# Joining the tiled stages of a Nyströmformer attention: R, A and both C v groups in one stage, R and C v in one PSUM bank, denominators earlier, G in two stages, u of two batches in one tile

## The chip, the cores and the metric

One core of one Trainium2 chip. The metric is the device time of one execution in microseconds (us). Runs of a program on one core are called slow when they lie over 1.5% above the fastest of the same kernel, the others called fast. "Span" is the time between the first and the last instruction of the profiled execution, some 1 to 2 us under its device time.

The engines: TensorE (PE, with its weight loads as PEld), VectorE (DVE), ScalarE (ACT), GpSimd (POOL), SyncE (SP, which here only issues transfers). Matmuls write into PSUM; "bank" is used here for 512 fp32 columns of it, the size of the code's `small` and `acc` tiles. "Start to start" below means from the start of one group of matmuls to the start of the next, so that waits and entries are included.

## The reference, cut to what matters

```python
# q, k, v: (8 batches, 8 heads, 576, 64)
q_lm = q.reshape(B, H, 32, 18, D).mean(axis=3)        # landmarks; k_lm alike
A  = softmax(q @ k_lm.T);  Bm = softmax(q_lm @ k_lm.T);  C = softmax(q_lm @ k.T)
Z  = Bm.T / (norm1(Bm) * norminf(Bm))
for _ in range(6):
    Z = 2 * Z - Z @ Bm @ Z                            # approximate inverse
x = (A @ Z @ C @ v), heads side by side               # (4608, 512)
out = ((x @ w1) * (x @ w2)) @ w3 @ w_out              # d_ff 1024
```

## The kernel before: the parts that matter

w3 and w_out are folded into one matrix `w34` at the start, and the attention of batch 0 is woven into that fold. After it, batch b does its up products (`g` against the normalised A: 8 `j`, two products each) and its down products ("chunks", `ab` against `w34`), and the attention of batch b+1 is woven in between: a Python generator, one stage per `yield`. The order of the matmuls is set by hand, and the timelines below show TensorE running them in that order, so a stage is a run of small matmuls between two runs of large ones. Most stages use the array as several small tiles (`tile_position`); up and down products use it whole. Counts of matmuls are those of the trace, in which an fp32 matmul call appears as two instructions (the 8 calls of R are x16 in the timelines below).

```python
def big():    return psp.tile([128, 2, 512], FP32, name="big", bufs=3)    # two PSUM banks each
def small():  return psp.tile([128, 512], FP32, name="small", bufs=1)     # one bank
def acc():    return psp.tile([128, 512], FP32, name="acc", bufs=1)       # one bank

# ... inside attention(st, bank); bank is small for batch 0, acc later ...
psR = bank()
# R: 16 matmuls of 32x32 into psR
for qd in range(2):                        # four VectorE reads of R in all
    nc.vector.tensor_scalar(out=sz_[:, qd, 0:32], in0=psR[:, 32*qd:32*qd+32], ...)
    nc.vector.scalar_tensor_tensor(out=tz_[:, qd, :], in0=psR[:, 32*qd:32*qd+32], ...)
scores_a(0)
yield
scores_a(1)

def cv(qd, es, psV):
    for r in range(6):
        for h in range(4): nc.tensor.matmul(psV[32*h:32*h+32, 0:64], ects[qd]..., vt...)   # L305
    for h in range(4): nc.tensor.matmul(psV[32*h:32*h+32, 64:65], es..., ones...)          # L310
    nc.vector.reciprocal(out=rcr, in_=psV[:, 64:65])
    nc.vector.tensor_scalar(out=sz_[:, qd, 32:96], in0=psV[:, 0:64], scalar1=rcr, ...)

cv(0, es0, small())
yield
cv(1, es1, bank())
yield
# ... (helpers cut: denominators() fills one half of a big(), inverted() and mixed()
#      turn it into rmix, the reciprocals of A's denominators; normalise() multiplies A by it)
for it in range(6):
    # 16 matmuls of the inverse, copies by VectorE (tz_, sz_)
    if it == 1: psS = denominators()
    elif it in (2, 3, 4): inverted(it - 2)
    elif it == 5: rmix = mixed()
    yield
# psZ, zt
normalise(0, rmix)
yield
normalise(1, rmix)
for n in range(2):
    for w in range(2):
        # G: 16 matmuls of 64x512, evicted by ScalarE or VectorE
        yield
```

The later loads are issued per batch: at its start four transposing loads (`turn_all`) and, behind them on the same queue, v as one block of 1152 KB; after the up products q and k, on GpSimd's queue.

The softmax here doesn't subtract the row's maximum and nothing guards it: scores larger than these inputs give would overflow.

Of the kernel before, what the change touches and what calls it, by code (L numbers as in the profile page):

```python
# [31 lines left out]
def kernel(  # L32
# [145 lines left out]
    def attention(st, bank=None):  # L178
# [102 lines left out]
                                 func=AXF.Exp, scale=SCALE / GRP)  # L281
            eat.append(e)

        psR = bank()
        for qd in range(2):
            for h in range(4):
                sl = slice(32 * h, 32 * h + 32)
                nc.tensor.matmul(psR[sl, 32 * qd:32 * qd + 32], bt[sl, qd, :], bt[sl, qd, :],
                                 start=True, stop=True, tile_position=(32 * h, 32 * h))
        sz_ = pz.tile([128, 2, 96], FP32, name="sz_")  # L290
        tz_ = pz.tile([128, 2, 32], FP32, name="tz_")
        for qd in range(2):
            nc.vector.tensor_scalar(out=sz_[:, qd, 0:32], in0=psR[:, 32 * qd:32 * qd + 32],
                                    scalar1=nrn[:, qd:qd + 1], scalar2=None, op0=ALU.mult)
            nc.vector.scalar_tensor_tensor(
                out=tz_[:, qd, :], in0=psR[:, 32 * qd:32 * qd + 32], scalar=nrn[:, qd:qd + 1],
                in1=eye2[:, qd, :], op0=ALU.mult, op1=ALU.add)
        scores_a(0)
        yield
        scores_a(1)  # L300

        def cv(qd, es, psV):
# [11 lines left out]
            nc.vector.tensor_scalar(out=sz_[:, qd, 32:96], in0=psV[:, 0:64],  # L314
                                    scalar1=rcr[:, 0:1], scalar2=None, op0=ALU.mult)


        cv(0, es0, small())
        yield
        cv(1, es1, bank())  # L320
        yield


        ahat = []
        psS = None

        def denominators():
            ps = big()
            for qd in range(2):
                for c in range(4):  # L330
                    nc.tensor.matmul(ps[32 * c:32 * c + 32, 0, 0:QS],
                                     onesq[:, qd].rearrange("p a b h -> p (a b h)"),
                                     eat[qd][:, QS * c:QS * (c + 1)],
                                     start=(qd == 0), stop=(qd == 1), tile_position=(0, 32 * c))
            return ps

        def inverted(i):
            sl = slice(QS // 3 * i, QS // 3 * (i + 1))
            nc.vector.reciprocal(out=psS[:, 1, sl], in_=psS[:, 0, sl])

        def mixed():
            rr = psS[:, 1, 0:QS]
            rhi = pat.tile([128, QS], FP16, name="rhi", bufs=1)
            nc.vector.tensor_copy(out=rhi, in_=rr)
            rmix = pat.tile([128, QS], FP16, name="rmix")
            nc.vector.scalar_tensor_tensor(out=rmix, in0=rhi, scalar=lomask[:, 0:1], in1=rr,
                                           op0=ALU.mult, op1=ALU.add)
            return rmix

        def normalise(qd, rmix):  # L350
            psD = big()
            for c in range(4):
                nc.tensor.matmul(psD[:, c // 2, QS * (c % 2):QS * (c % 2) + QS],  # L353
                                 selc[:, qd, c, :], rmix[:, :], start=True, stop=True)
            a = pat.tile([128, 2, HS], FP16, name="ahat", bufs=4)
            nc.vector.tensor_tensor(out=a, in0=eat[qd].rearrange("p (c s) -> p c s", c=2),  # L356
                                    in1=psD[:, :, 0:HS], op=ALU.mult)
            ahat.append(a)


        for it in range(6):
            last = it == 5
            psI = big()
            o = 32 if last else 0
            for h in range(4):
                for qd in range(2):
                    sl = slice(32 * h, 32 * h + 32)
                    t = h ^ qd
                    nc.tensor.matmul(psI[32 * t:32 * t + 32, qd, o:96], tz_[sl, qd, :],  # L369
                                     sz_[sl, qd, o:96], start=True, stop=True,  # L370
                                     tile_position=(32 * h, 32 * t))
            if not last:
                tz_ = pz.tile([128, 2, 32], FP32, name="tz_")
                nc.vector.tensor_tensor(out=tz_, in0=psI[:, :, 0:32], in1=eye2, op=ALU.add)
                sz_ = pz.tile([128, 2, 96], FP32, name="sz_")
                nc.vector.tensor_copy(out=sz_, in_=psI[:, :, 0:96])
            else:
                xd = pz.tile([128, 2, 64], FP32, name="xd")
                nc.vector.tensor_copy(out=xd, in_=psI[:, :, 32:96])
            if it == 1:  # L380
                psS = denominators()
            elif it in (2, 3, 4):
                inverted(it - 2)
            elif it == 5:
                rmix = mixed()
            yield
        psZ = small()
        for qd in range(2):
# [5 lines left out]
        nc.scalar.activation(out=zt[:, 0], in_=pzv, func=AXF.Copy, scale=-ZS)  # L394
        nc.vector.scalar_tensor_tensor(out=zt[:, 1], in0=pzv, scalar=-ZS, in1=zt[:, 0],
                                       op0=ALU.mult, op1=ALU.subtract)
        normalise(0, rmix)
        yield
        normalise(1, rmix)
        st["ahat"] = ahat  # L400


        g = st["g"] = pat.tile([128, 2, 2, DF], FP16, name="gt")
        for n in range(2):
            for w in range(2):
                psG = big()
                fs = slice(512 * n, 512 * n + 512)
                for i in range(2):
                    for h in range(4):
                        for qd in range(2):  # L410
                            rs = slice(64 * qd, 64 * qd + 64)
                            nc.tensor.matmul(psG[32 * h:32 * h + 32, qd, :], zt[rs, i, h, :],  # L412
                                             wup[rs, h, w, fs], start=(i == 0), stop=(i == 1),
                                             tile_position=(64 * qd, 32 * h))
                if w == 0:
                    nc.scalar.activation(out=g[:, :, w, fs], in_=psG, func=AXF.Copy, scale=1.0 / ZS)  # L416
                else:
                    nc.vector.tensor_scalar(out=g[:, :, w, fs], in0=psG, scalar1=1.0 / ZS,  # L418
                                            scalar2=None, op0=ALU.mult)
                yield  # L420

    def up(st, j, w):
        p = big()
# [6 lines left out]
            nc.scalar.copy(out=st["a_sb"], in_=p[:, :, 0:HS])  # L430
        else:
            nc.vector.tensor_tensor(  # L432
                out=st["ab"][:, j, :].rearrange("p (c s) -> p c s", c=2),
                in0=st["a_sb"], in1=p[:, :, 0:HS], op=ALU.mult)


    rows = out.rearrange("(b p g) f -> b g p f", b=B, g=6)

    def down(srcs, half, hold, bank):
        if half == 0:  # L440
            hold["ps"] = bank()
        pso = hold["ps"]
        for j in range(4 * half, 4 * half + 4):
            o = 0
            for _, ab, s0, sz in srcs:
                nc.tensor.matmul(pso[o:o + sz, :], ab[:, j, s0:s0 + sz], w34[:, j, :],  # L446
                                 start=(j == 0), stop=(j == 7),
                                 tile_position=(0, o))
                o += sz
        if half == 1:  # L450
            o_sb = po.tile([128, DM], FP32, name="o_sb")
            nc.scalar.activation(out=o_sb, in_=pso[:, :], func=AXF.Copy,  # L452
                                 scale=1.0 / (X64 * X64))
            o = 0
            for b, _, s0, sz in srcs:
                while sz:
                    gi, p0 = divmod(s0, NP)
                    n = min(sz, NP - p0)
                    nc.sync.dma_start(out=rows[b, 2 * (gi % 3) + gi // 3, p0:p0 + n, :],
                                      in_=o_sb[o:o + n, :])  # L460
                    o, s0, sz = o + n, s0 + n, sz - n


    def fold(pf, wof, w3f, wsp):
# [58 lines left out]
    with tc.tile_pool(name="pf", bufs=2) as pf:  # L523
# [19 lines left out]
        load_wout(2, nc.scalar)  # L543
        load_w3(1, 1)

        warm = pf.tile([128, 512], FP16, name="warm", bufs=1)
        nc.vector.memset(warm, 0.0)
        psw = big()
        for _ in range(10):
            nc.tensor.matmul(psw[:, 0, :], warm[:, 0:128], warm, start=True, stop=True)  # L550

        nc.gpsimd.tensor_copy(out=gate, in_=wof[1][:, 0, 0:1])
        load_qk(sts[0], 0)
# [25 lines left out]
        load_w3(5)  # L579
        steps(fd, 4)  # L580
        at = attention(sts[0])
        for n, m in enumerate((2, 2, 2, 2, 2, 2, 2, 1, 1, 1, 1, 1, 1, 1, 2, 2, 2, 2, 2, 1)):
            steps(at)
            if n == 3:
                load_w3(6)
# [7 lines left out]
            steps(fd, m)  # L593
        steps(at, 30)
        steps(fd, 64)
    pab = ctx.enter_context(tc.tile_pool(name="pab", bufs=3))
    at = attention(sts[1], acc)


    for b in range(B):  # L600
        st = sts[b]
        ab = st["ab"] = pab.tile([128, 8, S], FP16, name="ab")
        if b + 2 < B:
            turn_all(b + 2)
            load_v(sts[b + 2], b + 2)
        if b % 2 == 0:
            chunks = [[(b, ab, 128 * t, 128)] for t in range(4)]
        else:
            chunks = [[(b - 1, sts[b - 1]["ab"], 512, 64), (b, ab, 0, 64)]]
            chunks += [[(b, ab, 64 + 128 * t, 128)] for t in range(4)]  # L610
        for j in range(8):
            up(st, j, 0)
            steps(at, (0, 0, 1, 1, 1, 1, 1, 2)[j] if b == 0 else 1)
            up(st, j, 1)
        if b + 3 < B:
            load_qk(sts[b + 3], b + 3)
        if b + 2 < B:
# [4 lines left out]
        nd = 2 * len(chunks)  # L622
        for n in range(nd):
            bank = (lambda: big()[:, 0, :]) if n // 2 % 2 else acc
            down(chunks[n // 2], n % 2, hold, bank)
            steps(at, 2 if n == 6 and nd == 8 or b == 0 and n > 3 else 1)
        steps(at, 30)
        steps(nxt)
        at = nxt


# [28 lines left out]
```

## Time and profile before

| | before |
|---|---|
| device time, median (lowest to highest) | 296.15 us (295.37 to 296.77), 3 runs |
| span of the profiled run | 294.9 us |
| two batches of the main loop (up products of batch 2 to those of batch 4) | 56.07 us |
| TensorE waits marked "issue" | 0.40 us, once |

The first fence is from the page of the kernel before: the span, the busy time and its share for each engine, the chain of work that ended last by engine.

```profile
span 294.9 us, 9448 instructions
...
PE 277.5 (94%) x4026; PEld 152.7 (52%) x4026; DVE 174.1 (59%) x442; ACT 123.7 (42%) x199; POOL 141.7 (48%) x184
...
PE 82%; DVE 9%; ACT 6%; issue 2%; DVEq 0%; ACTq 0%
...
q8 instruction: 31, 0.51, 0.7%
```

TensorE bounds it (busy 94% of the span, 82% of the chain). But the ends of matmuls are modelled, so busy time also covers short waits (below, R is listed with 0.33 us and the next group starts 0.26 after it); start-to-start times are the better measure. The next fence is the PE timeline of the kernel before, in the batch that starts at 190.8 us: start, duration, engine, line, operands, array tile, shape, count, and in brackets an idle time with what ended it.

```profile
196.48 0.33 PE L288 MATMUL acc<-bt 32*32 32x32 f32 x16
196.74 0.32 PE L274 MATMUL big<-qkT,lm 64*32 64x288 f16 x8
196.99 1.15 PE L426 MATMUL big<-ahat,gt 128*128 128x288 f16 x8
198.07 0.32 PE L274 MATMUL big<-qkT,lm 64*32 64x288 f16 x8
198.32 0.88 PE L305 MATMUL small<-vt,ect 96*32 96x64 f32 x48
199.01 0.22 PE L310 MATMUL small<-ones,es 96*32 96x1 f32 x8
199.16 1.15 PE L426 MATMUL big<-ahat,gt 128*128 128x288 f16 x8
200.25 0.88 PE L305 MATMUL acc<-vt,ect 96*32 96x64 f32 x48
200.94 0.22 PE L310 MATMUL acc<-ones,es 96*32 96x1 f32 x8
201.09 1.15 PE L426 MATMUL big<-ahat,gt 128*128 128x288 f16 x8
...
210.17 1.04 PE L446 MATMUL acc<-w,ab 128*128 128x512 f16 x4
211.14 0.44 PE L389 MATMUL small<-bmbd,xd 128*64 128x128 f32 x4
...
211.77 1.03 PE L446 MATMUL acc<-w,ab 128*128 128x512 f16 x4
212.63 0.41 PE L353 MATMUL big<-rmix,selc 128*128 128x144 f16 x4
212.98 0.62 PE L412 MATMUL big<-wup,zt 64*32 64x512 f16 x16
213.53 1.04 PE L446 MATMUL big<-w,ab 128*128 128x512 f16 x4
```

Two things to see. Four down products (L446) take 0.97 us before a tiled group and 0.86 before one that uses the whole array: an entry into tiled work cost about 0.10 us. So it is throughout the main loop of this trace, from 80 us on: 0.95 to 0.99 us in 47 places before tiled groups, 0.86 to 0.88 in 9 before whole-array ones. And R with A0, A1 with the first C v, and the second C v are three stages: 0.51, 1.09 and 0.84 us, without any wait, plus three entries.

The last fence is from the list of PE's waits (line and what it waited for: total us, times, longest).

```profile
PE big L426 <- ACT a_sb L430: 1.7, 8, 0.2
PE acc L199 <- ACT lm L188: 1.4, 6, 0.3
PE big L369 <- issue: 0.4, 1, 0.4
```

### The profile page before, as it was taken

How to read it: one execution, taken by the hardware profiler on the slowest of the kernel's cores; microseconds unless marked ns; L12 is line 12 of the kernel's file. 1: busy time of each engine (PE TensorE's matmuls, PEld its weight loads, DVE VectorE, ACT ScalarE, POOL GpSimd, SP SyncE). 2: the span in 40 equal slices, each digit the busy share in tenths (PEclk: the TensorE clock that was granted, in tenths of full speed). 3: DMA queues.
4: the chain of work that ended last, by engine and by line, in shares of the span. 5: the costliest groups of instructions: out<-in, count | busy, mean ns of one | idle time of the engine just before them, and what ended most of it. 6: DMA issues, size and time to landing. Idle time of an engine off the chain costs nothing.

```text
span 294.9 us, 9448 instructions
## 1 busy us (share of the span) xinstructions
PE 277.5 (94%) x4026; PEld 152.7 (52%) x4026; DVE 174.1 (59%) x442; ACT 123.7 (42%) x199; POOL 141.7 (48%) x184
## 2 busy tenths in 40 slices
PE   8799789999999899999999999999999999999993
PEld 3355346544575357436743764376457435744641
DVE  7843733374474676656765765476666665665720
ACT  2114234215272366146525732573266236625531
POOL 1705405097049929942993599059909931500000
PEclk9799979999999999999999999999999999999999
DMA  7899999919956849947996999389949532012124
GB/s 238 279 235 242 219 259 259 182 35 178 175 133 87 186 104 186 210 132 111 175 227 165 146 224 189 100 167 203 221 116 169 119 107 71 4 37 74 37 65 113
DMA packets 61385, 45.56 MB, mean 154 GB/s; under 512 B 34976, under 2 KB 53408, under 8 KB 61344
## 3 DMA queue, kind: packets, MB, share of 16 engines
q1 hardware_dynamic: 46896, 31.86, 49.2%
q0 software_dynamic: 13632, 11.54, 25.0%
q10 hardware_dynamic: 816, 1.57, 1.5%
q8 instruction: 31, 0.51, 0.7%
q14 instruction: 10, 0.08, 0.1%
HBM read 38.80 MB, written 9.44 MB: 164 GB/s over the span
## 4 chain that ended last, share of the span: by engine, by line
PE 82%; DVE 9%; ACT 6%; issue 2%; DVEq 0%; ACTq 0%
PE big L426 17%; PE acc L446 13%; PE acc L490 12%; PE big L446 10%; PE big L412 6%; DVE ab L432 4%; PE big L369 4%; ACT a_sb L430 3%; PE small L305 2%; PE big L477 2%; PE small L490 2%; PE acc L305 2%; PE big L224 2%; PE big L550 2%; PE big L353 1%
## 5 line engine op out<-in xcount | busy, mean ns | idle before, releaser
L426 PE MATMUL big<-ahat,gt 128*128 128x288 f16 x512 | 74.1, 286 | 2.5 <-ACT a_sb L430 1.7
L432 DVE TENSOR_TENSOR ab<-a_sb,big 128x576 f16<-128x576 f16 x64 | 48.0, 750 | 19.6 <-PE big L426 8.4
L426 PEld LDWEIGHTS <-gt 128*128 128x128 f16 x512 | 47.1, 98 | 19.1 <-issue 4.1
L430 ACT CAST a_sb<-big 128x576 f16<-128x576 f32 x64 | 41.0, 640 | 36.7 <-PE big L426 35.9
L235 POOL TENSOR_TENSOR t<-ect 96x384 f32<-96x384 f32 x16 | 15.9, 994 | 79.3 <-ACT ect L228 78.6
L490 PE MATMUL acc<-wsp,w3t 128*128 128x512 f16 x168 | 43.4, 394 | 5.4 <-DVE w3t L483 2.7
L446 PE MATMUL acc<-w,ab 128*128 128x512 f16 (+1 forms) x192 | 41.0, 382 | 0.1
L446 PEld LDWEIGHTS <-ab 128*128 128x128 f16 (+1 forms) x320 | 24.0, 100 | 32.7 <-issue 9.8
L446 PE MATMUL big<-w,ab 128*128 128x512 f16 x128 | 32.8, 381 | 0.2 <-DVE ahat L356 0.2
L490 PEld LDWEIGHTS <-w3t 128*128 128x128 f16 x192 | 18.4, 101 | 25.9 <-issue 6.7
L166 POOL TENSOR_TENSOR tr<-qkT 128x768 f32<-128x768 f16 x15 | 24.6, 1642 | 11.5 <-DMA qkT<-qkn 6.6
L418 DVE TENSOR_SCALAR gt<-big 128x1024 f16<-128x1024 f32 x16 | 19.6, 1225 | 17.9 <-PE big L412 17.9
L452 ACT ACTIVATE o_sb<-acc 128x512 f32<-128x512 f32 x20 | 11.9, 597 | 38.5 <-PE acc L446 35.7
L167 POOL TENSOR_TENSOR tr<-tr,qkT 128x768 f32<-128x768 f32 x15 | 24.6, 1641 | 1.2
L483 DVE SCALAR_TENSOR_TENSOR w3t<-big,w3t 128x512 f16<-128x512 f32 x16 | 11.1, 691 | 18.9 <-ACT w3t L482 18.9
L482 ACT ACTIVATE w3t<-big 128x512 f16<-128x512 f32 x16 | 9.5, 596 | 25.6 <-PE big L477 20.7
L416 ACT ACTIVATE gt<-big 128x1024 f16<-128x1024 f32 x16 | 16.4, 1024 | 7.9 <-PE big L412 7.9
L412 PE MATMUL big<-wup,zt 64*32 64x512 f16 x512 | 19.3, 381 | 0.0
L452 ACT ACTIVATE o_sb<-big 128x512 f32<-128x512 f32 x16 | 9.6, 597 | 21.8 <-PE big L446 21.8
L228 ACT ACTIVATE ect<-big 96x768 f32<-96x768 f32 x16 | 12.9, 807 | 3.3 <-PE big L224 2.9
L356 DVE TENSOR_TENSOR ahat<-eat,big 128x576 f16<-128x576 f16 x16 | 11.9, 749 | 1.2 <-PE big L353 1.2
L172 POOL TENSOR_TENSOR o<-o,tr 128x256 f32<-128x256 f32 x15 | 12.0, 800 | 1.2
(313 smaller groups left out, 358.5 us busy)
## 6 DMA issues: line engine op xcount, KB each, us to landing
vt<-in_v_dram SPq DMA_DIRECT2D x8, 1152.0 KB, 8.7
qkn<-in_k_dram POOLq DMA_DIRECT2D x8, 576.0 KB, 10.5
qkn<-in_q_dram POOLq DMA_DIRECT2D x8, 576.0 KB, 13.2
out_dram<-o_sb SPq DMA_DIRECT2D x24, 192.0 KB, 2.3
w3f<-in_moe_w_dram SPq DMA_DIRECT2D x6, 512.0 KB, 8.0
out_dram<-o_sb SPq DMA_DIRECT2D x24, 128.0 KB, 2.3
wup<-in_moe_w_dram POOLq DMA_DIRECT2D x4, 512.0 KB, 18.4
wof<-in_moe_w_out_dram ACTq DMA_DIRECT2D x3, 512.0 KB, 7.5
```

The source lines that it names most:

```text
L166: eng.tensor_tensor(out=tr, in0=x[:, :, 0, :], in1=x[:, :, 1, :], op=ALU.add)
L167: eng.tensor_tensor(out=tr, in0=tr, in1=x[:, :, 2, :], op=ALU.add)
L235: nc.gpsimd.tensor_tensor(out=t3[0:NP], in0=e[:, :, 0:3, :], in1=e[:, :, 3:6, :], op=ALU.add)
L412: nc.tensor.matmul(psG[32 * h:32 * h + 32, qd, :], zt[rs, i, h, :], wup[rs, h, w, fs], start=(i == 0), stop=(i == 1), tile_position=(64 * ...
L416: nc.scalar.activation(out=g[:, :, w, fs], in_=psG, func=AXF.Copy, scale=1.0 / ZS)
L418: nc.vector.tensor_scalar(out=g[:, :, w, fs], in0=psG, scalar1=1.0 / ZS, scalar2=None, op0=ALU.mult)
L426: nc.tensor.matmul(p[:, c, 0:HS], st["g"][:, qd, w, 128 * j:128 * j + 128], st["ahat"][qd][:, c, :], start=(qd == 0), stop=(qd == 1))
L430: nc.scalar.copy(out=st["a_sb"], in_=p[:, :, 0:HS])
L432: nc.vector.tensor_tensor(out=st["ab"][:, j, :].rearrange("p (c s) -> p c s", c=2), in0=st["a_sb"], in1=p[:, :, 0:HS], op=ALU.mult)
L446: nc.tensor.matmul(pso[o:o + sz, :], ab[:, j, s0:s0 + sz], w34[:, j, :], start=(j == 0), stop=(j == 7), tile_position=(0, o))
L452: nc.scalar.activation(out=o_sb, in_=pso[:, :], func=AXF.Copy, scale=1.0 / (X64 * X64))
L490: nc.tensor.matmul(psW[j][:, :], turned[j, c // 4][:, a, c % 4, :], wsp[:, b, c, :], start=(c == 0 and a + b == 0), stop=(c == 7 and a == 1))
```

## The change

Its intent: fewer changes between whole-array and tiled matmuls. R, A and both C v become one stage. R and both C v share one `small` bank (`psX`) with the denominators and their reciprocals (the scores of A stay in `big`); the denominators go beside the first inverse step; the normalisations beside the fifth and sixth; G runs in two stages; `ab` of two batches is one tile, so a straddling chunk (64 rows of one batch and 64 of the next) needs no column tiles. The stage counts between the large products are adapted.

```diff
-        psR = bank()
+        psX = small()
...
-                nc.tensor.matmul(psR[sl, 32 * qd:32 * qd + 32], bt[sl, qd, :], bt[sl, qd, :],
+                nc.tensor.matmul(psX[sl, 140 + 32 * qd:172 + 32 * qd], bt[sl, qd, :], bt[sl, qd, :],
...
         scores_a(0)
-        yield
         scores_a(1)
...
-        cv(0, es0, small())
+        cv(0, es0, psX)
+        cv(1, es1, psX[:, 72:137])
         yield
-        cv(1, es1, bank())
-        yield
... denominators() writes psX[:, 208:352], the reciprocals go to psX[:, 352:496]
-            if it == 1:
-                psS = denominators()
-            elif it in (2, 3, 4):
-                inverted(it - 2)
-            elif it == 5:
-                rmix = mixed()
+            if it == 0:
+                denominators()
+            elif it < 4:
+                inverted(it - 1)
+                if it == 3:
+                    rmix = mixed()
+            else:
+                normalise(it - 4)
             yield
... (psZ, zt)
-        normalise(0, rmix)
         yield
-        normalise(1, rmix)
... (in G: the yield moves from the inner to the outer loop)
-    pab = ctx.enter_context(tc.tile_pool(name="pab", bufs=3))
+    pab = ctx.enter_context(tc.tile_pool(name="pab", bufs=2))
... one ab of 2 * S columns for two batches; down() takes 128 columns of it
-            steps(at, (0, 0, 1, 1, 1, 1, 1, 2)[j] if b == 0 else 1)
+            steps(at, (0, 0, 1, 1, 1, 1, 0, 1)[j] if b == 0 else (1, 1, 1, 1, 0, 1, 0, 0)[j])
... warm-up: 20 matmuls of 256 columns for 10 of 512; other stage counts
```

More of the change, by code (lines that the diff above doesn't have):

```diff
@@ L292, in attention @@
         for qd in range(2):
-            nc.vector.tensor_scalar(out=sz_[:, qd, 0:32], in0=psR[:, 32 * qd:32 * qd + 32],
+            psR = psX[:, 140 + 32 * qd:172 + 32 * qd]
+            nc.vector.tensor_scalar(out=sz_[:, qd, 0:32], in0=psR,
                                     scalar1=nrn[:, qd:qd + 1], scalar2=None, op0=ALU.mult)
             nc.vector.scalar_tensor_tensor(
-                out=tz_[:, qd, :], in0=psR[:, 32 * qd:32 * qd + 32], scalar=nrn[:, qd:qd + 1],
+                out=tz_[:, qd, :], in0=psR, scalar=nrn[:, qd:qd + 1],
                 in1=eye2[:, qd, :], op0=ALU.mult, op1=ALU.add)
         scores_a(0)
-        yield
         scores_a(1)
@@ L315, in cv @@
                                     scalar1=rcr[:, 0:1], scalar2=None, op0=ALU.mult)
-        cv(0, es0, small())
+        cv(0, es0, psX)
+        cv(1, es1, psX[:, 72:137])
         yield
-        cv(1, es1, bank())
-        yield
-        ahat = []
-        psS = None
         def denominators():
-            ps = big()
             for qd in range(2):
                 for c in range(4):
-                    nc.tensor.matmul(ps[32 * c:32 * c + 32, 0, 0:QS],
+                    nc.tensor.matmul(psX[32 * c:32 * c + 32, 208:208 + QS],
                                      onesq[:, qd].rearrange("p a b h -> p (a b h)"),
@@ L334, in denominators @@
                                      start=(qd == 0), stop=(qd == 1), tile_position=(0, 32 * c))
-            return ps
+        rr = psX[:, 352:352 + QS]
         def inverted(i):
             sl = slice(QS // 3 * i, QS // 3 * (i + 1))
-            nc.vector.reciprocal(out=psS[:, 1, sl], in_=psS[:, 0, sl])
+            nc.vector.reciprocal(out=rr[:, sl], in_=psX[:, 208 + sl.start:208 + sl.stop])
         def mixed():
-            rr = psS[:, 1, 0:QS]
             rhi = pat.tile([128, QS], FP16, name="rhi", bufs=1)
@@ L348, in mixed, with normalise @@
             return rmix
-        def normalise(qd, rmix):
+        ahat = st["ahat"] = []
+        def normalise(qd):
             psD = big()
@@ L396, in attention @@
                                        op0=ALU.mult, op1=ALU.subtract)
-        normalise(0, rmix)
         yield
-        normalise(1, rmix)
-        st["ahat"] = ahat
         g = st["g"] = pat.tile([128, 2, 2, DF], FP16, name="gt")
@@ L419, in attention @@
                                             scalar2=None, op0=ALU.mult)
-                yield
+            yield
     def up(st, j, w):
@@ L432, in up, with down @@
             nc.vector.tensor_tensor(
-                out=st["ab"][:, j, :].rearrange("p (c s) -> p c s", c=2),
+                out=st["ab"][:, j, st["t0"]:st["t0"] + S].rearrange("p (c s) -> p c s", c=2),
                 in0=st["a_sb"], in1=p[:, :, 0:HS], op=ALU.mult)
     rows = out.rearrange("(b p g) f -> b g p f", b=B, g=6)
-    def down(srcs, half, hold, bank):
+    def down(ab, b0, t0, half, hold, bank):
         if half == 0:
@@ L443, in down @@
         for j in range(4 * half, 4 * half + 4):
-            o = 0
-            for _, ab, s0, sz in srcs:
-                nc.tensor.matmul(pso[o:o + sz, :], ab[:, j, s0:s0 + sz], w34[:, j, :],
-                                 start=(j == 0), stop=(j == 7),
-                                 tile_position=(0, o))
-                o += sz
+            nc.tensor.matmul(pso[:, :], ab[:, j, t0:t0 + 128], w34[:, j, :],
+                             start=(j == 0), stop=(j == 7))
         if half == 1:
@@ L454, in down @@
             o = 0
-            for b, _, s0, sz in srcs:
-                while sz:
-                    gi, p0 = divmod(s0, NP)
-                    n = min(sz, NP - p0)
-                    nc.sync.dma_start(out=rows[b, 2 * (gi % 3) + gi // 3, p0:p0 + n, :],
-                                      in_=o_sb[o:o + n, :])
-                    o, s0, sz = o + n, s0 + n, sz - n
+            while o < 128:
+                gi, p0 = divmod((t0 + o) % S, NP)
+                n = min(128 - o, NP - p0)
+                nc.sync.dma_start(out=rows[b0 + (t0 + o) // S, 2 * (gi % 3) + gi // 3, p0:p0 + n, :],
+                                  in_=o_sb[o:o + n, :])
+                o += n
     def fold(pf, wof, w3f, wsp):
@@ L544 @@
         load_w3(1, 1)
-        warm = pf.tile([128, 512], FP16, name="warm", bufs=1)
+        warm = pf.tile([128, 256], FP16, name="warm", bufs=1)
         nc.vector.memset(warm, 0.0)
         psw = big()
-        for _ in range(10):
-            nc.tensor.matmul(psw[:, 0, :], warm[:, 0:128], warm, start=True, stop=True)
+        for _ in range(20):
+            nc.tensor.matmul(psw[:, 0, 0:256], warm[:, 0:128], warm, start=True, stop=True)
         nc.gpsimd.tensor_copy(out=gate, in_=wof[1][:, 0, 0:1])
@@ L581 @@
         at = attention(sts[0])
-        for n, m in enumerate((2, 2, 2, 2, 2, 2, 2, 1, 1, 1, 1, 1, 1, 1, 2, 2, 2, 2, 2, 1)):
+        for n, m in enumerate((2, 2, 2, 2, 2, 1, 1, 1, 1, 1, 1, 2, 3, 3)):
             steps(at)
@@ L601 @@
         st = sts[b]
-        ab = st["ab"] = pab.tile([128, 8, S], FP16, name="ab")
+        if b % 2 == 0:
+            ab = pab.tile([128, 8, 2 * S], FP16, name="ab")
+        st["ab"], st["t0"] = ab, S * (b % 2)
         if b + 2 < B:
@@ L605 @@
             load_v(sts[b + 2], b + 2)
-        if b % 2 == 0:
-            chunks = [[(b, ab, 128 * t, 128)] for t in range(4)]
-        else:
-            chunks = [[(b - 1, sts[b - 1]["ab"], 512, 64), (b, ab, 0, 64)]]
-            chunks += [[(b, ab, 64 + 128 * t, 128)] for t in range(4)]
+        chunks = range(0, 512, 128) if b % 2 == 0 else range(512, 2 * S, 128)
         for j in range(8):
             up(st, j, 0)
-            steps(at, (0, 0, 1, 1, 1, 1, 1, 2)[j] if b == 0 else 1)
+            steps(at, (0, 0, 1, 1, 1, 1, 0, 1)[j] if b == 0 else (1, 1, 1, 1, 0, 1, 0, 0)[j])
             up(st, j, 1)
+        steps(at, 1)
         if b + 3 < B:
@@ L624 @@
             bank = (lambda: big()[:, 0, :]) if n // 2 % 2 else acc
-            down(chunks[n // 2], n % 2, hold, bank)
-            steps(at, 2 if n == 6 and nd == 8 or b == 0 and n > 3 else 1)
+            down(ab, b - b % 2, chunks[n // 2], n % 2, hold, bank)
+            steps(at)
         steps(at, 30)
-        steps(nxt)
         at = nxt
```

## The prediction

> **What bounds the kernel now.** TensorE: the page's busy line gives PE 277.5 of 294.9 us (94%), the chain of waits is 82% PE, 9% DVE, 6% ACT. Two batches of the main loop take 56.1 us (PE timeline). Busy time hides two things. Tiled stages alternate with full-array matmuls: four output matmuls take 0.87 us, start to next, before a full-array group and 0.97 before a tiled one, so an entry costs 0.10; sixteen G matmuls take 0.56, thirty-two 0.99, so a join saves 0.13. [...] And there are waits for evictions: 0.17 us at each of the first two inverse steps, 0.35 at the landmark copy, 0.37 after the first C scores.
>
> **What the change does, per batch,** counted start to start in the PE timeline:
> 1. R, A0, A1, C v 0, C v 1 took 2.74 us in three stages with their entries. Joined, without waits, about 2.34: -0.4.
> 2. R and both C v groups now share one bank. [...] I expect C v 0 to wait for VectorE's reads of R, and C v 1 for those of C v 0. No trace shows this yet. From durations: R's reads end 1.13 us after R starts, PE is through A earlier: wait 0.55. C v 0's reads end 0.80 after its last sums start: wait 0.79. Together +1.34; stage about 3.7 us.
> 3. G in two stages, not three or four: -0.32.
> 4. The first normalisation moves beside the fifth inverse step, the reciprocals' split into the fourth. VectorE needs 2.0 us from that step's start (copies, 0.46, 0.30, 0.36); PE arrives after 1.63: +0.4.
> 5. Denominators no longer hold a double bank, and no steps follow the last up products: the two 0.17 waits go: -0.3.
> 6. Landmarks, B and C scores move by one up product: about 0.7 us of waits before and after: 0.
> 7. Full-array output for the straddling rows: -0.05; the last such chunk 1.85 to 1.73. The warm-up does the same work.
>
> Sum: +0.7 for each of seven interleaved batches, +5. The first attention, woven into the weight fold, has the same waits and about 0.6 in the fourth step: +1. All on PE, so on the critical path: 302. The shared-bank wait is inferred; without it the same sum gives about 292.5. Weighed: **300.5 us, 80% range 292 to 304.5; faster by over 2% 0.10, within 2% 0.57, slower by over 2% 0.33.**
>
> **What would show it.** In the list of waits: C v matmuls waiting for VectorE (reads of R; scaling of C v), about 0.5 and 0.8 us, eight times each. In the PE timeline: the joined stage near 3.7 us with two gaps; normalisation matmuls 0.4 late behind the mixed reciprocals; G as two groups of 32 at 0.99; the last two up products without gaps; two batches in 57 to 58 us. Right on saving, wrong on waits: joined stage 2.3 to 2.5 us, two batches near 55.
>
> **What would make it wrong.** C v not ordered against VectorE's reads in its bank (about 292.5). Evictions around the C scores releasing earlier than worked out. The normalisation's wait absorbed by a late fourth step. DMA: busy up to 0.9 in some slices, though no PE wait on it shows.

-0.4, +1.34, -0.32, +0.4, -0.3, 0 and -0.05 make +0.7 per batch, seven times +5; with +1 for the first attention, 302 us from the 296.15 measured before. The wait in step 2 was an assumption; its size, +1.34 us, is an estimate from durations in the trace before.

## The result, and the profile after

| | before | after |
|---|---|---|
| device time, median | 295.76 us, 4 runs | 309.12 us (307.52 to 309.85), 4 runs |
| ratio | | 1.0441 (95% interval 1.0389 to 1.0492) |
| span of the profiled run | 294.9 us | 307.8 us |
| PE busy | 277.5 us | 277.8 us |
| PE waits marked "issue" | 0.40 us | 3.95 us |

A ratio is the mean time of one kernel's fast runs over that of the other's fast runs of the same rounds, so it is not quite the ratio of the medians quoted here. The change is slower by 4.4%.

From the page of the kernel after:

```profile
span 307.8 us, 9392 instructions
...
PE 277.8 (90%) x4004; PEld 155.4 (50%) x4004; DVE 174.0 (57%) x442; ACT 122.4 (40%) x199; POOL 141.2 (46%) x184
...
PE 79%; DVE 11%; ACT 5%; issue 3%; POOL 1%; ACTq 0%; DVEq 0%
```

TensorE has hardly more work; it waits more. The PE timeline of the kernel after, in the same batch as above:

```profile
207.81 0.33 PE L288 MATMUL small<-bt 32*32 32x32 f32 x16
208.07 0.55 PE L274 MATMUL big<-qkT,lm 64*32 64x288 f16 x16
208.99 0.88 PE L305 MATMUL small<-vt,ect 96*32 96x64 f32 x48 [0.37 <-DVE tz__3387 L296]
209.69 0.22 PE L310 MATMUL small<-ones,es 96*32 96x1 f32 x8
210.55 0.88 PE L305 MATMUL small<-vt,ect 96*32 96x64 f32 x48 [0.64 <-DVE sz__3386 L314]
211.24 0.22 PE L310 MATMUL small<-ones,es 96*32 96x1 f32 x8
211.39 2.72 PE L419 MATMUL big<-ahat,gt 128*128 128x288 f16 x20
...
219.51 0.40 PE L363 MATMUL big<-sz__3606,tz__3604 32*32 32x96 f32 x16
220.39 0.42 PE L348 MATMUL big<-rmix,selc 128*128 128x144 f16 x4 [0.48 <-DVE rmix L339]
...
224.44 1.06 PE L405 MATMUL big<-wup,zt 64*32 64x512 f16 x32
225.43 1.04 PE L437 MATMUL big<-w,ab 128*128 128x512 f16 x4
```

The joined stage takes 3.58 us (207.81 to 211.39), with two waits for VectorE in it. The timeline of VectorE of the kernel after, at the same time, shows what they are:

```profile
208.21 0.25 DVE L294 TENSOR_SCALAR sz__3386<-small,nrn 128x32 f32<-128x32 f32 x1
...
208.70 0.24 DVE L296 SCALAR_TENSOR_TENSOR tz__3387<-small,nrn,eye 128x32 f32<-128x32 f32 x1
210.00 0.17 DVE L313 RECIPROCAL rcr<-small 128x1 f32<-128x1 f32 x1 [1.06 <-PE small L310]
210.21 0.28 DVE L314 TENSOR_SCALAR sz__3386<-small,rcr 128x64 f32<-128x64 f32 x1
```

The last read of R ends at 208.94, the first C v starts at 208.99; the last read of the first C v ends at 210.49, the second C v starts at 210.55. Neither matmul needs what was read: it writes other columns of the same bank. `psX` is one tile that fills one bank, so no run tells an order kept for the tile from one kept for the bank.

From the list of PE's waits of the kernel after (the lines for L305 come once per attention, with other buffer numbers):

```profile
PE big L348 <- DVE rmix L339: 3.9, 8, 0.6
...
PE small L324 <- issue: 2.5, 1, 2.5
PE big L419 <- ACT a_sb L423: 1.6, 7, 0.2
...
PE small L305 <- DVE sz__1216 L314: 0.6, 1, 0.6
...
PE acc L437 <- issue: 0.6, 1, 0.6
...
PE small L310 <- issue: 0.6, 1, 0.6
```

The wait for the landmark copy (L199, 1.4 us before) is gone. New are the waits for the mixed reciprocals and those marked "issue", in which PE waited for nothing that the profile shows. The longest of these lies at 152.9 to 155.4 us. The view by stretches shows what followed (per engine busy time and count, then PEclk, DMA share, GB/s; the stretches are 3 us each):

```profile
153.00:156.00 3.00, 0.57 (x3) 0.21 (x3) 0.70 (x3) 0.00 (x0) 2.70 (x6) 1.00 1.29 200
156.00:159.00 3.00, 3.00 (x23) 0.75 (x21) 0.86 (x3) 0.00 (x0) 2.92 (x2) 0.52 1.22 188
159.00:162.00 3.00, 3.00 (x49) 1.09 (x55) 1.72 (x6) 0.60 (x1) 2.62 (x5) 0.91 0.36 101
```

After the wait, TensorE was granted about half its clock (0.52 in the stretch from 156 to 159 us) for 3.4 us, from 156.1 to 159.5 in the trace's clock records. Two down-product groups and two inverse steps took 4.08 us there and 2.59 us in the next batch, so this one wait cost 2.5 + 1.5 us.

Where the 12.9 us of span went, read from both PE timelines:

| part | before | after | difference |
|---|---|---|---|
| until the landmark product of batch 0 | 41.0 | 40.4 | -0.6 |
| first attention in the weight fold, until the first up product | 36.9 | 39.0 | +2.1 |
| seven batches with an attention in them | 194.4 | 206.0 | +11.6 |
| last batch | 22.5 | 22.3 | -0.2 |

Of the 11.6 us, 3.3 are more issue waits (3.7 against 0.4), 1.5 the halved clock, and 6.8 are left: about 1.0 us per batch.

### The profile page after: what moved, and what is told of

Read it like the earlier page. It is cut to its first block, busy times and chain, and to the rows that moved or that the text cites. A ratio compares the mean times of both kernels' runs of the same rounds, so it can differ in the third digit from the quotient of the medians.

```text
span 307.8 us, 9392 instructions
## 1 busy us (share of the span) xinstructions
PE 277.8 (90%) x4004; PEld 155.4 (50%) x4004; DVE 174.0 (57%) x442; ACT 122.4 (40%) x199; POOL 141.2 (46%) x184
## 4 chain that ended last, share of the span: by engine, by line
PE 79%; DVE 11%; ACT 5%; issue 3%; POOL 1%; ACTq 0%; DVEq 0%
PE big L419 20%; PE acc L437 12%; PE acc L478 11%; PE big L437 8%; PE big L405 5%; PE big L363 5%; PE small L305 4%; ACT a_sb L423 2%; PE big L348 2%; PE small L478 2%; PE big L465 2%; PE big L538 1%; PE big L224 1%; DVE ab L425 1%; PE small L183 1%
## 5 line engine op out<-in xcount | busy, mean ns | idle before, releaser
L419 PEld LDWEIGHTS <-gt 128*128 128x128 f16 x512 | 48.1, 98 | 22.5 <-issue 8.7
L437 PE MATMUL acc<-w,ab 128*128 128x512 f16 x160 | 41.5, 389 | 0.6 <-issue 0.6
L437 PEld LDWEIGHTS <-ab 128*128 128x128 f16 x288 | 24.2, 98 | 33.0 <-issue 9.9
L305 PE MATMUL small<-vt,ect 96*32 96x64 f32 x768 | 14.0, 221 | 8.2 <-DVE sz__1216 L314 0.6
L405 PE MATMUL big<-wup,zt 64*32 64x512 f16 x512 | 17.1, 380 | 0.0
L305 PEld LDWEIGHTS small<-vt,ect 96*32 96x32 f32 x768 | 11.5, 110 | 10.6 <-POOL es L238 0.8
L228 ACT ACTIVATE ect<-big 96x768 f32<-96x768 f32 x16 | 12.9, 806 | 3.3 <-PE big L224 2.9
```

The source lines that it names most:

```text
L305: nc.tensor.matmul(psV[32 * h:32 * h + 32, 0:64], ects[qd][0:NP, h, r, :], vt[0:NP, 4 * qd + h, 64 * r:64 * r + 64], start=(r == 0), stop= ...
L405: nc.tensor.matmul(psG[32 * h:32 * h + 32, qd, :], zt[rs, i, h, :], wup[rs, h, w, fs], start=(i == 0), stop=(i == 1), tile_position=(64 * ...
L419: nc.tensor.matmul(p[:, c, 0:HS], st["g"][:, qd, w, 128 * j:128 * j + 128], st["ahat"][qd][:, c, :], start=(qd == 0), stop=(qd == 1))
L437: nc.tensor.matmul(pso[:, :], ab[:, j, t0:t0 + 128], w34[:, j, :], start=(j == 0), stop=(j == 7))
```

## The experiments

Three theories had to be told apart: (a) the shared bank makes TensorE wait for VectorE; (b) the joined stage is slow in itself; (c) the issue waits are late fetches of TensorE's instructions, held up by data traffic. The pages of the kernel before and of the kernel after list a DMA queue q8 of the kind "instruction" with 31 packets, 0.51 MB, thus 16 KB each. PE's 4004 matmuls and 4004 weight loads in the kernel after make 31.3 times 256; so one packet is taken here to bring the next 256 instructions of TensorE, called a block (an estimate from these counts), and its transfer a fetch. In the trace's transfer records of the kernel after, one such packet starts at 137.3 us of the span and the next only at 152.6, just before PE stands still (539 of PE's instructions started between 137.3 us and that wait); the transposing loads run from 140.8 to 147.8 and the block of v from 147.8 to 154.2. In neither kernel did a fetch start between 1.0 and 4.5 us after the start of a v block (a block takes 5 to 9 us); they lie just at its start or cluster at its end. Whether the transposing loads hold fetches up as well was not tested: of the six sets of them from 72 us on in the kernel after (6.7 to 7.6 us each), only two have a fetch that starts more than 1 us inside, at 2.0 and 5.2 us.

Counting the instructions supports this. Take PE's matmuls, weight loads and semaphore instructions of a trace in order: over all 17 profiles the timelines list 38 waits marked issue, of 0.2 to 3.7 us, and every one of them comes 193 or 194 instructions after a multiple of 256, with TensorE going on 2.2 to 3.5 us after a packet of q8 had started. So they are read as waits for the next block of instructions; the experiments below are about why a block comes late.

The runs of one call shared the runs of the kernel before; its medians in the five calls were 296.68, 296.40, 295.21, 297.41 and 295.55 us. The kernel after was not run again beside them, so "of 309" below compares over calls.

### e1: banks of their own

```diff
         psX = small()
+        own = (lambda: big()[:, 0, :]) if bank is small else bank
+        psRR = own()                     # R here
...
-        cv(1, es1, psX[:, 72:137])
+        cv(1, es1, own())
```

> The changed kernel, but R and the second C v group get banks of their own (the single bank, or a half of a double one for the first attention); the stage stays joined. Theory (the shared bank makes TensorE wait for VectorE): the waits of 0.37 and 0.64 us before the C v matmuls vanish in all eight attentions, the joined stage falls from 3.58 to 2.3-2.5 us start to start, and the time from about 309 by 8 to 10 us to 299-301 us. Rival (the joined stage is slow in itself, [...] by late sums on GpSimd): stage above 3.3 us, time above 306.

Measured: correct, 303.35 us (302.22 to 304.0), ratio to before 1.0222. The waits before L305 are gone. The mended stage is shown from e3 below: 2.32 us. So (a) holds and (b) falls. The gain was 6 us and not the 8 to 10 expected; this run had 5.4 us of issue waits, two of over 2 us: the profile's list shows them at other places than in the kernel after.

### e2: the normalisations one stage later

```diff
-            else:
-                normalise(it - 4)
+            elif it == 5:
+                normalise(0)
             yield
... after zt:
+        normalise(1)
         yield
```

> The changed kernel, but the two normalisations one stage later each (beside the sixth inverse step and behind the product with Z). Theory: the wait for the mixed reciprocals (3.9 us in all in the changed kernel) goes and nothing takes its place: 309 less 3 to 4 us, 305-306 us. Rival (the wait only moves, to VectorE work later in the chain): less than 1.5 us gained.

Measured: correct, 303.86 us (302.18 to 305.16), ratio 1.024. The wait for rmix is gone from the list and no wait of that kind took its place. The gain, 5 us, is above the 3.9 us of the waits; this profile also has 2.8 us of issue waits against 3.95, which is of the size of the excess.

### e3: both

> Both mendings together. If the two waits and nothing else made the changed kernel slow, the sum of both gains: 309 less 11 to 13.5 us, 295.5-298 us, within 1% of the kernel before. If instruction waits of TensorE (3.95 us marked issue in the profile after, 0.40 before) belong to the change, it stays 3 to 5 us above that.

Measured: correct, 298.29 us over four runs, of which two (299.87 and 300.89) counted as slow; the fast ones were 296.71 and 295.15, ratio 0.9976 (0.991 to 1.0042): the same as before. The PE timeline of e3, in the batch that starts at 160 us:

```profile
168.19 0.33 PE L290 MATMUL acc<-bt 32*32 32x32 f32 x16
168.44 0.55 PE L274 MATMUL big<-qkT,lm 64*32 64x288 f16 x16
168.93 0.88 PE L307 MATMUL small<-vt,ect 96*32 96x64 f32 x48
169.62 0.22 PE L312 MATMUL small<-ones,es 96*32 96x1 f32 x8
169.68 0.86 PE L307 MATMUL acc<-vt,ect 96*32 96x64 f32 x48
170.36 0.22 PE L312 MATMUL acc<-ones,es 96*32 96x1 f32 x8
170.51 2.72 PE L422 MATMUL big<-ahat,gt 128*128 128x288 f16 x20
```

2.32 us, no wait: the stage that the change intended. Still e3 gained nothing over the kernel before, and it had 5.3 us of issue waits. That left (c).

### e4: the kernel after without the later loads of v (wrong results on purpose)

```diff
-            load_v(sts[b + 2], b + 2)
+            sts[b + 2]["vt"] = sts[b]["vt"]
```

> Wrong results on purpose: the changed kernel without the loads of v for batches 2 to 7 (the old tiles are read again), all TensorE work unchanged. Theory (the four waits marked issue are late fetches of TensorE's instructions, held up behind the loads of v): the issue waits fall from 3.95 us to under 1 us, the dip of TensorE's speed after the long one goes, and the time falls by 3 to 5.5 us to 304-306 us. Rival (they belong to the program order and not to DMA traffic): issue waits above 2.5 us at the same places, time within 1.5 us of 309.

Measured: 303.92 us (301.9 to 305.11), ratio 1.0222, so about 5 us less. Its output is wrong, which doesn't matter for the time. Its list of PE's waits has one line marked issue, a little over the 1 us expected, in the weight fold at 59 us, where the early loads still run:

```profile
PE big L363 <- issue: 1.2, 1, 1.2
```

None is left in the main loop, and the view of the clock shows no dip there (no four down products take over 1.1 us; 1.89 followed the long wait of the kernel after). TensorE's program was the same and the transposing loads still ran: the issue waits of the main loop, 3.7 us in the kernel after and none here, went with the traffic of v.

### e5 and e7: v in four parts between the transposes, in the kernel after and in the kernel before

```diff
                 transposes(sts[b], t, range(h0, h0 + 4))
+                if b > 1:
+                    h = 4 * (1 - t) + h0 // 2
+                    load_v(sts[b], b, slice(h, h + 2))
```

> The changed kernel, correct results, the same bytes: each later load of v is cut into four of two heads, one behind each of the four transposing loads, instead of one block behind them all. In every trace so far the fetches of TensorE's instructions start just before or at the end of the block of v, never in its middle. Theory (a block of v holds a fetch up): the issue waits in the main loop (3.7 us in the profile after) fall to under 1 us, 309 less 3 to 5 us, 304-306 us. Rival (the run without v gained because less data moved, not because of the block): the issue waits stay, time within 1.5 us of 309.

e5 measured: correct, 305.94 us (305.14 to 306.08), ratio 1.0326. Issue waits in the main loop 1.4 us instead of 3.7: they shrank but did not fall under 1.

> The kernel before with the load of v in four parts alone. It shows 0.4 us of issue waits, so the theory gives 0 to 1 us of gain (295.5-297 us). If the cut itself is worth several us in any kernel (rival): under 294 us, and then it says nothing of the change.

e7 measured: correct, 296.47 us, two of six runs slow, ratio 0.9994. The cut is worth nothing where there is nothing to wait for. e5 moved the same bytes as the kernel after and still lost most of the waits in the loop, so less data is not the whole reason for e4's gain.

### e6: e3 with v in four parts

> Own banks, later normalisations and the load of v in four parts, together. e3 ran at 298 us with 5.3 us of issue waits, so without those of the main loop (3.8 us): 293.5-295.5 us, 0.5 to 1.5% under the kernel before. If the waits of TensorE for instructions only move to another place: 297-299 us.

Measured: correct, 294.77 us (one of six runs slow), ratio 0.9956 (0.9897 to 1.0014). Issue waits 4.1 us, one of 2.36 us at 116 us. The time fits the first expectation, the profile the second: between the transposes is not a safe place for v.

### e8: two parts of the change alone, on the kernel before

G in two stages and `ab` of two batches in one tile, as in the diff of the change; everything else as before.

> The kernel before with only two parts of the change: G in two stages, and u of two batches in one tile. From the profile after, G is 0.1-0.2 us per batch shorter and one or two entries of 0.10 us fewer, the straddling chunks 0.05: in all 1.5 to 3 us off, 294-295.5 us. If these parts cost something, 297 or more.

Measured: correct, 293.5 us (290.98 to 293.88), ratio 0.9892 (0.9841 to 0.9943), no wait marked issue. These parts are good by themselves, by about 1%. Batches took 26.5 and 28.2 us in turn, against 26.7 and 29.4 in the kernel before.

### e9: e3 with v on GpSimd's queue, still at the start of the batch

> e3 (own banks, later normalisations) with the later loads of v issued from GpSimd's queue, on which the loads of q and k already travel: in all traces fetches of TensorE's instructions do start in the middle of those. Theory (only the block of v on the hardware queue, behind the transposes, holds fetches up): issue waits after 100 us fall from 3.8 us to under 0.6 us, 298 less 3 to 4.5 us, 293.5-295 us. If any block of v holds a fetch up, whatever queue: issue waits above 2 us remain, 296 or more.

Measured: correct, 295.4 us (294.13 to 295.87), ratio 0.9987. That fetches start in the middle of the loads of q and k shows in the kernel after, for instance 3.0 us into those from 120.9 to 129.1 us. After 100 us one issue wait remained, of 3.7 us at 118 us, when v and the transposes of one batch ran together; the batches from 163 us on had none and took 54.1 us for two. A mixed outcome: another queue alone does not remove the waits.

### e10: e3 with the program shifted by half a block

```diff
-        for _ in range(20):
-            nc.tensor.matmul(psw[:, 0, 0:256], warm[:, 0:128], warm, start=True, stop=True)
+        for _ in range(84):
+            nc.tensor.matmul(psw[0:32, 0, 0:64], warm[:, 0:32], warm[:, 0:64],
+                             start=True, stop=True, tile_position=(0, 0))
```

> e3 with 128 more instructions on TensorE in the warm-up (84 small matmuls for 20 larger, about the same time), so that every later 256-instruction block begins half a block elsewhere in the program. If the instruction waits come by chance of where blocks end: their places change and their sum differs by over 2 us from 5.3 us (either way), and the time with it. If they come from the joined stage (288 instructions in 2.3 us[...]): 4 to 6 us again, beside or soon after joined stages, 297-300 us.

Measured: correct; three of six runs slow, the fast ones 298.29 to 299.99, ratio 1.0132. The profile fell in a slow run: five issue waits, 11.4 us, none where e3 had its own. So where blocks end decides where the waits fall: e1, e3, e6, e9 and e12 all wait at one and the same place of the program, in the C v near 116 us, where the shifted e10 does not, and three of the five waits of e10 come again in e15, shifted alike. A slow run's sum is not compared with e3's. The fast runs are longer too (mean 299.4 us, e3's fast ones 295.9), but no profile of one was kept.

### e11: e8 with the joined stage, banks of its own

> e8 (the kernel before with G in two stages and u of two batches in one tile, 293.5 us, no issue waits) with R, A and both C v joined in one stage, each in a bank of its own. In e3 that stage took 2.32 us where three stages with their entries took 2.74. So 0.4 us times eight less: 290-291 us, if the join costs nothing else. If joining brings the instruction waits of e1 and e3 (5.3 us): 293-297 us with issue waits above 2 us in the profile.

Measured: correct, 296.62 us (294.46 to 297.51), ratio 1.0027, issue waits 1.8 us. It is no clean test: with my distribution of stages, up products waited 2.6 us for VectorE's `ab`, and the up products of a batch took 9.3 us against 8.8. What joining is worth on e8 stays open.

### e12: e3 with v moved away from the transposes

```diff
             load_qk(sts[b + 3], b + 3)
         if b + 2 < B:
+            load_v(sts[b + 2], b + 2, nc.gpsimd)     # was: sync queue, behind turn_all
... and for batch 1 likewise, in the weight fold
```

> e3 with every later load of v moved off the transposes: on GpSimd's queue behind the loads of q and k, issued when the up products of a batch are done (and for batch 1 in the weight fold likewise). In the profile of e9 the batches without an instruction wait took 54.1 us per pair, against 56.1 in the kernel before. Theory (the instruction waits are fetches held up by v meeting the transposes): issue waits under 1 us in all, seven batches at that pace, 289-292 us, faster than the kernel before by 1 to 2%. If fetches are merely late behind any dense traffic: issue waits of 2 us or more in the profile, 293-297 us.

Measured: correct, 291.23 us (289.06 to 291.94), ratio 0.9813 (0.9763 to 0.9864): the fastest of all, 1.9% under the kernel before. Against e3 both the queue and the time of the loads changed; against e9, on the same queue (ratio 0.9987), only the time and the load of batch 1. The one line marked issue in its list of PE's waits:

```profile
PE acc L312 <- issue: 0.7, 1, 0.7
```

The clock was halved nowhere in the main loop (no four down products took over 1.1 us there).

### e13, e14, e15: the same shift in kernels without the joined stage, and in e12

> The kernel before with 128 more instructions on TensorE in the warm-up (74 small matmuls for 10 larger, about the same time). If the joined stage makes the instruction waits: under 1 us of them here too, 295-298 us, the same. If they come from where 256-instruction blocks end: over 2 us of them, and 298-301 us.

> e8 (kernel before with only G in two stages and u in one tile, no issue wait seen) with the same 128 more instructions. Joined stage as the cause: under 1 us of issue waits, 292-295 us. Block ends as the cause: over 2 us, 295-298 us.

> e12 (joined, own banks, v off the transposes, 0.7 us of issue waits, 291 us) with the same 128 more instructions. If moving v is a cure and not luck of alignment: under 1.5 us of issue waits, 290-293 us. Else like the shifted e3: over 4 us, 295 us or more.

Measured, all correct: e13 297.28 us, ratio 1.005; e14 296.03 us, ratio 0.9986; e15 293.97 us, ratio 0.9944 (0.9888 to 0.9999). e13 had one issue wait of 1.4 us and e14 one of 1.7 us, both in the C v of the weight fold, and none in the main loop. Their sums lie between my two expectations; read for the main loop alone, they follow the first. e15 had 3.75 us, 2.1 of them in the main loop: moving v lessens the waits, it does not rule them out, and e15 missed both of its expectations. The shift also took back part of what e8 and e12 had gained: by the medians e14 lies 0.4% and e15 1.1% under e13, the kernel before with the same shift, where e8 and e12 lay 1.1% and 1.9% under the kernel before.

Issue waits of PE in the main loop, from the profiles (e10, profiled in a slow run, is left out):

| kernel | joined stage | v | us |
|---|---|---|---|
| before, e7, e8, e13, e14 | no | behind or between the transposes | 0.4, 0, 0, 0, 0 |
| after, e1, e2, e3 | yes | behind the transposes | 3.7, 4.7, 2.8, 3.8 |
| e11 | yes | behind the transposes | 1.8 |
| e5, e6 | yes | between the transposes | 1.4, 2.6 |
| e9 | yes | with the transposes, other queue | 3.7 |
| e12, e15 | yes | after the transposes | 0.7, 2.1 |
| e4 | yes | not loaded | 0 |

All five kernels without the joined stage, at several alignments, have next to none; all joined ones that load v have some. The joined stage holds 144 matmuls and 144 weight loads, over one block of 256, in 2.3 us at its fastest. Whether this rate of use makes a fetch come late was not shown: no run varied the rate alone. For the longest wait of the kernel after, the traces speak against it: without the wait, the block of 256 before it took 5.3 us, and the block of the same number took 5.3 us in e8, where no wait came. What differed was the fetch: it began 5.0 us after TensorE had entered that block, near the end of the block of v, against 1.7 us in e8 and 0.7 in e4. So that wait, the largest of the 3.7 us, is put down to when the block end met the load of v. Why the joined kernels meet it so often stays open.

Slower work after a wait was not seen in the kernel after alone. In the main loop it followed every issue wait of 1.89 us or more and none of 1.26 or less: after 2.31 us in e1, 2.36 in e6 and 3.71 in e9, twenty up products (`ahat` against `gt`) took 4.19, 4.29 and 4.11 us, and 2.72 after 1.26 us in e3; after 1.89 us in e2 and 2.02 in e1, four down products took up to 1.89 us, and about 1.04 elsewhere. In the weight fold it followed a wait of 1.50 us in e3 (three `wsp` products 1.46 us) and not one of 1.50 us at the same place in e6 (0.82).

## Why the prediction was wrong

The prediction said 300.5 us, 292 to 304.5; it was 309.1.

- **Step 2, the shared bank: right, size included.** Predicted waits 0.55 and 0.79 us, stage about 3.7 us; start to start they are 0.43 (A takes 0.92 us where e3 has 0.49) and 0.80 (from the first sums, L310, to the second C v 0.86 us where e3 has 0.06), stage 3.58. e1 and e3 take the sharing away and the waits go; unshared, 2.32 us were measured and 2.34 predicted. In the trace of the kernel after, reads end at 208.94 us and the next write starts at 208.99.
- **Step 4, the reciprocals: right.** Predicted +0.4; measured 0.44 to 0.48 in the loop, 0.62 in the fold. e2 removes it.
- **Step 5: right.** Inverse steps took 2.28 us per batch before and 2.47 after, with 0.48 of the new wait in it: -0.3.
- **Step 3, G: too favourable.** G itself went from 2.10 or 2.22 to 2.00 us. With the entries, which fall into the down products around it (+0.09 in even, -0.06 in odd batches), about -0.14 per batch stands for the -0.32 predicted.
- **Step 6, "0":** the up products needed two entries less (0.2 us) but went only from 8.78 to 8.74, so about +0.16 of new waits.
- **"The first attention ... +1":** it was +2.1, with waits of 0.53 (the sums of C v not yet there from GpSimd), 0.63, 0.62 and 0.23 us and ScalarE's evictions of the folded weights seen.
- **The sum, "All on PE, so on the critical path: 302":** this step failed most. It counted semaphore waits and matmul times, and left out that TensorE also waits for instructions, whose fetch came late behind v (in the kernel after at 152.6 us, near the end of the block of v from 147.8 to 154.2, some 15 us after the fetch before it). Those waits (3.3 us more in the loop) and the halved clock after the longest (1.5 us) make 4.8 of the 7 us between 302 and 309. I had set DMA aside because "no PE wait on it shows"; the waits read here as late fetches are marked issue and not DMA. e4 and e5 show the term: without the v traffic, or with v cut, the kernel after runs at 304 to 306 us.
- **"Weighed: 300.5":** the shared-bank wait was put at less than certain, as no trace had shown it; this pulled the number 1.5 us below its own sum, and 0.33 was too little for "slower".

## What to carry to other kernels

Before joining small stages, list who reads each PSUM bank that they write: here a bank shared by successive matmul groups, as one tile, made a chain of TensorE and VectorE (1.2 us per batch), and banks of their own gave the intended 0.4 us back. Then look at which large transfers run beside the joined stage: waits marked "issue" are worth a look at the instruction queue's packets, and moving one load was worth 1.7% here (e9 to e12: ratio to the kernel before 0.9987 to 0.9813, fast runs alone). Parts of a change that is slow as a whole may still be good; run them alone (e8: 293.5 us). And repeat a gain of 1 or 2% with the program shifted by half a block: here the shift took part of it back (e14, e15).
